# Sparse attention and token mixing on one core: another order for the products of weights and values, and one integer addition per decoded weight

## The chip, the cores and the metric

The kernel runs on one core of one Trainium2 chip, in one launch. The metric is the device time of that core in microseconds. The engines of a core are named as in the profile: PE is TensorE's matrix products and PEld its weight loads, DVE is VectorE, ACT is ScalarE, POOL is GpSimd, SP is SyncE, which here only issues DMAs.

## The reference

Two layers follow one another. The first is attention over 4 batches x 8 heads, 768 tokens, 64 channels per head, with a mask in blocks of 32 tokens: a query block sees its neighbours, the first and the last block, and three sampled ones; the first and the last query block see everything.

```python
scores = scale * np.matmul(q, k.transpose(0, 1, 3, 2))
scores = np.where(mask, scores, -1000000000.0)
scores = scores - np.max(scores, axis=-1, keepdims=True)
attn = np.exp(scores)
attn = attn / (np.sum(attn, axis=-1, keepdims=True) + 1e-09)
return np.matmul(attn, v).astype(np.float32)
```

Its output, 4 x 768 x 512, goes into a token mix:

```python
theta = x @ w_theta
zr, zi = x * np.cos(theta), x * np.sin(theta)
y = w_tok_r @ zr + w_tok_i @ zi        # over tokens, per batch
u = x + y
return (u + np.maximum(u @ w_ch, 0.0)).astype(np.float32)
```

The four weight matrices of the token mix arrive as float64, the rest as float32.

## The kernel before, in words

**Attention** (`attention`). The batches are taken in two halves `bp` of two batches. Per half there are 26 units: four "wide" ones, for the first and last query block against all keys, then one for each query block `i` from 1 to 22, against 8 key blocks. The engines' work is written out by hand in program order (`tc.manual_schedule`), a software pipeline over units `n`: in the turn of unit n come the key gathering of n+2 (`gather_k`, GpSimd copies, line 243), the scores of n+1 (`scores`, line 282, TensorE, and row minima on VectorE, line 285), the exponentials of n+1 (line 294, ScalarE), the transposes of n (line 300, TensorE) and their copy out of PSUM (line 302, ScalarE), and at every odd `i` the products of weights and values of the pair before it (`values`, line 335), whose results VectorE normalises (lines 315 to 319, one output tile `xo`) and SyncE stores to DRAM as `xs` (line 348). Last in a turn stand the loads of values: a window `va` (line 262, two buffers) and by `gather_v` an indirect DMA that GpSimd issues into one of four buffers `vb` (line 265). Queues are served in this order.

`values` works on a pair of query blocks and 16 heads (b, e, p). A head takes three products into its 64 rows of PSUM tile `X`: for each of the two query blocks one with the values of its sampled blocks, `vb`, 32 columns of weights wide; then one for both blocks with the shared window `va`, 64 columns wide, added to the two. Which rows of PSUM, and so which columns of the array, a head uses depends on p: rows 0 to 63 for even p, 64 to 127 for odd p. Each float32 product appears in the trace as two records. For the wide units `values_wide` (line 392) sums six products per head, 64 columns wide, two heads (c = 0 and 1) per call.

**Decoding of the weights** (`Piece`, `Decoder`). The float64 weights are read as pairs of 32-bit words and turned into two float32r parts, `hi` and `lo`. In the attention there are 22 pieces of 128 x 512, later 8 of 128 x 256 for `w_ch`. A piece has three phases. Before them ScalarE's `start` (line 63) scales the high word, read as float32, without its sign. `bits` (lines 67 to 69, VectorE) clips it, shifts it and puts the sign back: a float32 with the high word's part of the mantissa. `rest` (lines 75 and 77, VectorE) cuts out that value's power of two and multiplies the low word by it. Then ScalarE rounds the first part to `hi` (line 80), and `low` (lines 83 and 84, VectorE) subtracts `hi` and adds the rest. `Decoder.ahead` puts ScalarE's parts and `Decoder.go` the others into a turn. `attention` spreads the 66 phases over the units: none for the first two, then by a weight of 1 for a block and 2 for a wide unit, 56 in all. The load of piece k+2 (two buffers `raw`) is issued after `low` of piece k. In the turn, `go` stands behind the key gathering and ahead of the stores and the loads of values.

**Token mix** (`token_mix`). 48 steps in which weights' products with tokens (lines 584 to 586, angles; 622 to 624, mixing; 645 to 647, last product) fill TensorE. Here a planner orders the instructions. The last eight pieces are decoded in steps 1 to 12, two phases a step.

Of the kernel before, what the change touches and what calls it, by code (L numbers as in the profile page):

```python
# [10 lines left out]
F32 = mybir.dt.float32  # L11
F32R = mybir.dt.float32r
I32 = mybir.dt.int32
U32 = mybir.dt.uint32
AF = mybir.ActivationFunctionType
# [15 lines left out]

WORD_LO = float(np.array([768 << 20], np.uint32).view(np.float32)[0])
WORD_HI = float(np.array([(1022 << 20) | 0xFFFFF], np.uint32).view(np.float32)[0])
SIGN_BIT = -(1 << 31)
EXP_BITS = -(1 << 23)


C1 = 6.28125  # L40
# [5 lines left out]
class Piece:  # L46
# [13 lines left out]

    def start(self):
        self.a = self.pool.tile([P, self.f], F32, tag="da", name=f"da_{self.name}", bufs=2)
        self.nc.scalar.activation(self.a, self.raw[:, :, 1].bitcast(F32), AF.Abs, scale=2.0**-16)

    def bits(self):
        nc, a, ai = self.nc, self.a, self.a.bitcast(I32)
        nc.vector.tensor_scalar(a, a, WORD_LO, WORD_HI, op0=ALU.max, op1=ALU.min)
        nc.vector.tensor_scalar(ai, ai, 4, 1, op0=ALU.logical_shift_left, op1=ALU.logical_shift_right)
        nc.vector.scalar_tensor_tensor(ai, self.raw[:, :, 1], SIGN_BIT, ai, op0=ALU.bitwise_and, op1=ALU.bitwise_or)

    def rest(self):

        nc = self.nc
        s = self.pool.tile([P, self.f], I32, tag="ds", name=f"ds_{self.name}")
        nc.vector.tensor_scalar(s, self.a.bitcast(I32), EXP_BITS, None, op0=ALU.bitwise_and)
        low = self.raw[:, :, 0]
        nc.vector.scalar_tensor_tensor(low.bitcast(F32), low.bitcast(U32), 2.0**-52, s.bitcast(F32), op0=ALU.mult, op1=ALU.mult)

    def high(self):
        self.nc.scalar.copy(self.hi, self.a)  # L80

    def low(self):
        self.nc.vector.tensor_tensor(self.a, self.a, self.hi.bitcast(F32), op=ALU.subtract)
        self.nc.vector.tensor_tensor(self.lo, self.a, self.raw[:, :, 0].bitcast(F32), op=ALU.add)


class Decoder:
# [20 lines left out]
    def go(self, n):  # L108
        for k in range(self.at, min(self.at + n, 3 * len(self.pieces))):
            piece = self.pieces[k // 3]  # L110
            (piece.bits, piece.rest, piece.low)[k % 3]()
            if k % 3 == 2 and k // 3 + 2 < len(self.pieces):
                self.pieces[k // 3 + 2].load(self.pool, self.queue)
        self.at += n

# [54 lines left out]
def attention(tc, qT, qE, kT, vr, sampled, xs, ident, pieces, follow):  # L170
# [9 lines left out]
    with ExitStack() as ctx, ExitStack() as early:  # L180
# [146 lines left out]
        def values(bp, i):  # L327
            x = st[bp, i]["X"] = sums_tile(f"{bp}_{i}")
            va = vas[((i - 1) // 2) % VA_BUFS]
            order = [(b, e, p) for b in range(2) for e in range(2) for p in range(4)]  # L330

            def weigh(b, e, p, c, u0, n, v, start, stop):
                r0 = 64 * (p % 2) + 32 * u0
                v0 = 65 * (8 * b + 4 * (p // 2) + 2 * e + p % 2)
                nc.tensor.matmul(  # L335
                    x[r0 : r0 + 32 * n, b, 2 * (p // 2) + e, :], pT_pair[:, 4 * c + 2 * e + b, p, u0 : u0 + n, :], v[:, v0 : v0 + 65],
                    start=start, stop=stop,
                )

            for b, e, p in order:  # L340
                for u in range(2):
                    weigh(b, e, p, 1, u, 1, vbs[(i - 1 + u) % VB_BUFS], True, False)
                weigh(b, e, p, 0, 0, 2, va, False, True)

        def finish(bp, i):
            xo = normalised(f"{bp}_{i}", st.pop((bp, i))["X"], 8)
# [38 lines left out]
        def values_wide(bp, b, pp, e):  # L385
            if (b, pp, e) == (0, 0, 0):
                xws[bp] = sums_tile(f"w{bp}")
            x, v = xws[bp], vws[bp, b, pp]
            for c in range(2):
                for k in range(6):  # L390
                    v0 = 130 * e + 65 * c
                    nc.tensor.matmul(
                        x[64 * c : 64 * c + 64, b, 2 * pp + e, :], pT_wide[:, e, k, 64 * c : 64 * c + 64], v[:, k, v0 : v0 + 65],
# [389 lines left out]
```

## Time and profile before

| | |
|---|---|
| median of three runs | 726.09 us (721.34 to 729.16) |
| the profiled execution's own time | 730.01 us |
| its span, first to last instruction | 728.2 us |
| mean granted TensorE clock | 0.962 |
| moved by DMA | 95.57 MB, mean 131 GB/s |

The page of a profile gives each engine's busy time, and rows of forty digits, one for each fortieth of the span (18.2 us): the busy share of an engine in tenths, the clock that TensorE was granted, the mean share of the 16 DMA engines. The table by stage has the same in numbers for chosen stretches; its columns are the stretch, its length, each engine's busy time with the number of instructions, clock, DMA share and GB/s. The chain in order of time follows the work that ended last: start, length, engine, output tile and line. Timeline rows have the start, the length, engine, line, operation, output and inputs and the count of records merged into the row; a bracket behind it is the idle time before it and what ended that. Group rows have line, engine, operation, operands, shapes and count, then the busy time in us and the mean of one in ns, then the idle time ahead of them. Matrix products overlap, so the length of one is not the time that it costs.

### The profile page before, as it was taken

How to read it: one execution, taken by the hardware profiler on the slowest of the kernel's cores; microseconds unless marked ns; L12 is line 12 of the kernel's file. 1: busy time of each engine (PE TensorE's matmuls, PEld its weight loads, DVE VectorE, ACT ScalarE, POOL GpSimd, SP SyncE). 2: the span in 40 equal slices, each digit the busy share in tenths (PEclk: the TensorE clock that was granted, in tenths of full speed). 3: DMA queues.
4: the chain of work that ended last, by engine and by line, in shares of the span. 5: the costliest groups of instructions: out<-in, count | busy, mean ns of one | idle time of the engine just before them, and what ended most of it. 6: DMA issues, size and time to landing. Idle time of an engine off the chain costs nothing.

```text
span 728.2 us, 16678 instructions
## 1 busy us (share of the span) xinstructions
PE 681.6 (94%) x6592; PEld 566.3 (78%) x6592; DVE 462.2 (63%) x1063; ACT 333.8 (46%) x708; POOL 133.5 (18%) x262
## 2 busy tenths in 40 slices
PE   5899999997979999999785999999999999999997
PEld 2666666664666666666574999999999999999997
DVE  3676667563268575766427887875668575855753
ACT  3454545453155354535334556543554355633530
POOL 1435444432204444534000000000000000000000
PEclk9999999997589999999898999999999999999999
DMA  8665655866256564654324432242113311121102
GB/s 312 216 206 171 193 192 176 268 187 241 70 178 207 159 198 155 204 189 143 106 63 142 110 95 57 81 125 65 54 42 113 102 62 57 43 77 62 41 0 87
DMA packets 71110, 95.57 MB, mean 131 GB/s; under 512 B 5240, under 2 KB 52984, under 8 KB 71032
## 3 DMA queue, kind: packets, MB, share of 16 engines
q1 hardware_dynamic: 64696, 71.08, 30.9%
q0 software_dynamic: 6336, 23.43, 10.3%
q8 instruction: 52, 0.85, 0.5%
q14 instruction: 26, 0.21, 0.1%
HBM read 81.90 MB, written 12.58 MB: 130 GB/s over the span
## 4 chain that ended last, share of the span: by engine, by line
PE 69%; DMA 12%; DVE 10%; ACT 5%; SPq 2%; issue 2%; DVEq 0%; ACTq 0%
PE X L335 22%; PE y L622 7%; PE y L623 7%; PE y L624 7%; PE T L300 5%; DMA xs<-xo 3%; PE S L282 3%; DMA out_dram<-of 3%; PE SW L365 3%; ACT pT L302 3%; PE h L586 2%; PE h L584 2%; PE h L585 2%; DMA kb<-in_kT_dram 2%; PE o L645 2%; PE o L646 2%
## 5 line engine op out<-in xcount | busy, mean ns | idle before, releaser
L335 PE MATMUL X<-va,pT 128*64 128x65 f32 x704 | 118.4, 251 | 0.0
L335 PE MATMUL X<-vb,pT 128*32 128x65 f32 x1408 | 114.3, 236 | 1.5 <-ACT pT L302 1.1
L243 POOL COPY kg<-kb 128x256 f32 (+2 forms) x202 | 88.2, 477 | 67.8 <-PE S L282 33.8
L335 PEld LDWEIGHTS X<-va,pT 128*64 128x64 f32 x704 | 68.8, 138 | 34.2 <-issue 2.8
L302 ACT COPY pT<-T 128x1024 f32<-128x1024 f32 x44 | 44.6, 1014 | 96.7 <-PE T L300 96.5
L294 ACT ACTIVATE P<-S,m 128x256 f32<-128x256 f32 x176 | 69.1, 479 | 39.6 <-DVE m L285 39.6
L335 PEld LDWEIGHTS X<-vb,pT 128*32 128x32 f32 x1408 | 54.1, 109 | 35.3 <-ACT pT L302 1.3
L285 DVE TENSOR_REDUCE m<-S 128x2 f32<-128x512 f32 x88 | 56.4, 682 | 24.6 <-PE S L282 24.5
L265 POOL DMA_INDIRECT vb<-in_vr_dram,rows x44 | 43.3, 985 | 140.4 <-PE X L335 133.6
L622 PE MATMUL y<-w_tok_r_hi,zh 128*128 128x384 f32 x192 | 65.1, 339 | 2.8 <-DVE xo L319 1.6
L584 PE MATMUL h<-w_theta_hi,xTh 128*128 128x256 f32 x192 | 57.2, 298 | 10.5 <-ACT xTh L575 10.5
L623 PE MATMUL y<-w_tok_r_lo,zh 128*128 128x384 f32 x192 | 64.4, 335 | 0.0
L624 PE MATMUL y<-w_tok_r_hi,zl 128*128 128x384 f32 x192 | 64.2, 335 | 0.0
L623 PE MATMUL y<-w_tok_i_lo,zh 128*128 128x384 f32 x192 | 64.2, 334 | 0.0
L622 PE MATMUL y<-w_tok_i_hi,zh 128*128 128x384 f32 x192 | 64.2, 334 | 0.0
L624 PE MATMUL y<-w_tok_i_hi,zl 128*128 128x384 f32 x192 | 61.3, 334 | 0.0
L586 PE MATMUL h<-w_theta_hi,xTl 128*128 128x256 f32 x192 | 56.8, 297 | 1.4 <-DVE xTl L576 1.4
L585 PE MATMUL h<-w_theta_lo,xTh 128*128 128x256 f32 x192 | 56.4, 294 | 0.0
L300 PE MATMUL T<-ident,P 128*128 128x128 f32 x352 | 49.0, 283 | 4.0 <-ACT pT L302 1.6
L300 PEld LDWEIGHTS T<-ident,P 128*128 128x128 f32 x352 | 38.6, 143 | 15.9 <-ACT pT L302 13.7
L282 PE MATMUL S<-kg,q 64*32 64x256 f32 x1408 | 48.9, 387 | 0.0
L315 DVE TENSOR_SCALAR sm<-X 128x8 f32<-128x8 f32 x22 | 3.6, 165 | 70.1 <-PE X L335 70.1
(127 smaller groups left out, 1354.6 us busy)
## 6 DMA issues: line engine op xcount, KB each, us to landing
xa<-xs SPq DMA_DIRECT2D x192, 64.0 KB
vw<-in_vr_dram SPq DMA_DIRECT2D x8, 780.0 KB
kb<-in_kT_dram SPq DMA_DIRECT2D x8, 768.0 KB
xr<-xs SPq DMA_DIRECT2D x96, 64.0 KB
out_dram<-of SPq DMA_DIRECT2D x32, 192.0 KB
va<-in_vr_dram SPq DMA_DIRECT2D x22, 260.0 KB
q<-in_qT_dram SPq DMA_DIRECT2D x22, 256.0 KB
xs<-xo SPq DMA_DIRECT2D x44, 128.0 KB
```

The costliest lines, as they stand in the source:

```text
L243: nc.gpsimd.tensor_copy(dst, blocks.rearrange("r g s f -> r s g f"))
L282: nc.tensor.matmul(sc[32 * p : 32 * p + 32, e, b, :], q[rows, b, p, :], keys[rows, :, :, 4 * b + p, :], start=True, stop=True)
L294: nc.scalar.activation(pt[:, e, b, :], sc[:, e, b, :], AF.Exp, bias=m[:, e, b : b + 1], scale=-1.0)
L300: nc.tensor.transpose(t[:, k, :], pt, ident)
L302: nc.scalar.copy(out, t.rearrange("r k (p q) -> r k p q", p=4) if len(out.shape) == 4 else t)
L335: nc.tensor.matmul(x[r0 : r0 + 32 * n, b, 2 * (p // 2) + e, :], pT_pair[:, 4 * c + 2 * e + b, p, u0 : u0 + n, :], v[:, v0 : v0 + 65], star ...
L584: nc.tensor.matmul(ps, hi[:, c, :], wh[:, c, :], start=c == 0, stop=False)
L585: nc.tensor.matmul(ps, hi[:, c, :], wl[:, c, :], start=False, stop=False)
L586: nc.tensor.matmul(ps, lo[:, c, :], wh[:, c, :], start=False, stop=c == 3)
L622: nc.tensor.matmul(acc, zh[:, dd], wh[:, j, tt], start=j == 0 and m == 0, stop=False)
L623: nc.tensor.matmul(acc, zh[:, dd], wl[:, j, tt], start=False, stop=False)
L624: nc.tensor.matmul(acc, zl[:, dd], wh[:, j, tt], start=False, stop=j == 5 and m == 1)
```

## The change

Three things are changed.

In `values` the 16 heads are taken in four groups of four (one e, one half of p, both b and both p in it). In a group come first the eight products 32 wide, then the four 64 wide. The products are the same. In `values_wide` the loops over c and k are swapped, so that the two heads alternate.

In `Piece` a float32 value is made whole before it is split. ScalarE's `start` scales the high word by another power of two and has a second pass that scales the low word and writes it as an integer `r`. `bits` clips, shifts once, and puts the sign into `r`. `rest` is one integer addition by GpSimd of the two. `high` rounds the sum as before, and `low` is one subtraction. So VectorE's lines 75, 77 and 83 go, and ScalarE and GpSimd get one operation each. `r` has one buffer.

The load of piece k+2 is issued after `bits` of piece k, since nothing reads the raw words behind it.

```diff
-WORD_LO = float(np.array([768 << 20], np.uint32).view(np.float32)[0])
-WORD_HI = float(np.array([(1022 << 20) | 0xFFFFF], np.uint32).view(np.float32)[0])
+WORD_LO = float(np.array([512 << 20], np.uint32).view(np.float32)[0])
+WORD_HI = float(np.array([(766 << 20) | 0xFFFFF], np.uint32).view(np.float32)[0])
 SIGN_BIT = -(1 << 31)
-EXP_BITS = -(1 << 23)
...
-        self.nc.scalar.activation(self.a, self.raw[:, :, 1].bitcast(F32), AF.Abs, scale=2.0**-16)
+        self.nc.scalar.activation(self.a, self.raw[:, :, 1].bitcast(F32), AF.Abs, scale=2.0**-48)
+        self.r = self.pool.tile([P, self.f], I32, tag="ds", name=f"ds_{self.name}")
+        self.nc.scalar.activation(self.r, self.raw[:, :, 0].bitcast(U32), AF.Copy, scale=2.0**-29)
 
     def bits(self):
-        nc, a, ai = self.nc, self.a, self.a.bitcast(I32)
+        nc, a, ai, r = self.nc, self.a, self.a.bitcast(I32), self.r
         nc.vector.tensor_scalar(a, a, WORD_LO, WORD_HI, op0=ALU.max, op1=ALU.min)
-        nc.vector.tensor_scalar(ai, ai, 4, 1, op0=ALU.logical_shift_left, op1=ALU.logical_shift_right)
-        nc.vector.scalar_tensor_tensor(ai, self.raw[:, :, 1], SIGN_BIT, ai, op0=ALU.bitwise_and, op1=ALU.bitwise_or)
+        nc.vector.tensor_scalar(ai, ai, 3, None, op0=ALU.logical_shift_left)
+        nc.vector.scalar_tensor_tensor(r, self.raw[:, :, 1], SIGN_BIT, r, op0=ALU.bitwise_and, op1=ALU.bitwise_or)
 
     def rest(self):
 
-        nc = self.nc
-        s = self.pool.tile([P, self.f], I32, tag="ds", name=f"ds_{self.name}")
-        nc.vector.tensor_scalar(s, self.a.bitcast(I32), EXP_BITS, None, op0=ALU.bitwise_and)
-        low = self.raw[:, :, 0]
-        nc.vector.scalar_tensor_tensor(low.bitcast(F32), low.bitcast(U32), 2.0**-52, s.bitcast(F32), op0=ALU.mult, op1=ALU.mult)
+        ai = self.a.bitcast(I32)
+        self.nc.gpsimd.tensor_tensor(ai, ai, self.r, op=ALU.add)
...
     def low(self):
-        self.nc.vector.tensor_tensor(self.a, self.a, self.hi.bitcast(F32), op=ALU.subtract)
-        self.nc.vector.tensor_tensor(self.lo, self.a, self.raw[:, :, 0].bitcast(F32), op=ALU.add)
+        self.nc.vector.tensor_tensor(self.lo, self.a, self.hi.bitcast(F32), op=ALU.subtract)
...
-            if k % 3 == 2 and k // 3 + 2 < len(self.pieces):
+            if k % 3 == 0 and k // 3 + 2 < len(self.pieces):
                 self.pieces[k // 3 + 2].load(self.pool, self.queue)
...
-            order = [(b, e, p) for b in range(2) for e in range(2) for p in range(4)]
-
...
-            for b, e, p in order:
-                for u in range(2):
-                    weigh(b, e, p, 1, u, 1, vbs[(i - 1 + u) % VB_BUFS], True, False)
-                weigh(b, e, p, 0, 0, 2, va, False, True)
+            for e in range(2):
+                for pp in range(2):
+                    heads = [(b, e, 2 * pp + c) for b in range(2) for c in range(2)]
+                    for head in heads:
+                        for u in range(2):
+                            weigh(*head, 1, u, 1, vbs[(i - 1 + u) % VB_BUFS], True, False)
+                    for head in heads:
+                        weigh(*head, 0, 0, 2, va, False, True)
...
-            for c in range(2):
-                for k in range(6):
+            for k in range(6):
+                for c in range(2):
```

## The prediction

> **What bounds the kernel now.** I read the page first: who is busy, when, and at which clock.
>
> ```profile
> span 728.2 us, 16678 instructions
> PE 681.6 (94%) x6592; PEld 566.3 (78%) x6592; DVE 462.2 (63%) x1063; ACT 333.8 (46%) x708; POOL 133.5 (18%) x262
> ...
> PEclk9999999997589999999898999999999999999999
> DMA  8665655866256564654324432242113311121102
> ...
> PE 69%; DMA 12%; DVE 10%; ACT 5%; SPq 2%; issue 2%; DVEq 0%; ACTq 0%
> ```
>
> TensorE owns the chain that ended last. The table by stage then says where that can change.
>
> ```profile
> core 0: us, PE busy (x) PEld busy (x) DVE busy (x) ACT busy (x) POOL busy (x), PEclk, DMA share, GB/s
> 0.00:47.90 47.90, 35.62 (x449) 23.66 (x450) 29.13 (x71) 22.18 (x34) 16.75 (x45) 0.96 0.75 250
> ...
> 231.50:343.40 111.90, 110.70 (x1589) 73.58 (x1585) 73.34 (x122) 53.72 (x106) 50.42 (x94) 1.00 0.57 180
> ...
> 400.00:500.00 100.00, 98.80 (x608) 97.60 (x607) 77.45 (x232) 54.17 (x136) 0.00 (x0) 0.98 0.32 90
> 500.00:728.20 228.20, 222.86 (x1390) 222.49 (x1389) 145.84 (x371) 100.42 (x238) 0.00 (x0) 1.00 0.20 62
> ```
>
> From 400 us on, the token mix keeps TensorE busy 98% of the time with matrix products that the change doesn't touch: 328 us stay. The attention before it is a loop over pairs of query blocks, and the chain in order of time shows one period of it.
>
> ```profile
> 243.91 8.15 PE X L335 x96
> 252.06 1.04 PE T L300 x8
> 253.18 1.02 ACT pT L302
> 254.24 1.09 PE T L300 x8
> 255.33 1.02 PE S L282 x32
> 256.36 8.15 PE X L335 x96
> ```
>
> A period is 12.44 us (256.36 less 243.91): 8.15 for the 96 records of L335 (48 products of weights and values, each float32 product two records) and 4.3 for transposes and scores, TensorE hardly waiting. There are nine such periods in each of the two halves, 18 together.
>
> **The order of the products.** Within L335 the timeline, in narrow windows, reads:
>
> ```profile
> 111.21 0.25 PE L335 MATMUL X<-vb,pT 128*32 128x65 f32 x2
> ```
> ```profile
> 111.21 0.31 PE L335 MATMUL X<-vb,pT 128*32 128x65 f32 x4
> 111.44 0.33 PE L335 MATMUL X<-va,pT 128*64 128x65 f32 x2
> 111.70 0.31 PE L335 MATMUL X<-vb,pT 128*32 128x65 f32 x4
> ```
>
> One head is four records 32 columns wide, then two records 64 wide, and takes 0.49 us (111.70 less 111.21): 0.23 for the first kind, 0.26 for the second. The two products 32 wide go to different columns of the array and run side by side (both started within the first row's 0.25 us, and its two records end by 0.25, though one lasts 0.236 by the row below). Then the next width waits until the array has run empty. That is a switch of width twice per head, 32 times in the 8.15 us. The rows that show what the array does without such switches:
>
> ```profile
> 204.28 1.44 PE L392 MATMUL Xw<-vw,pT 128*64 128x65 f32 x24
> 205.65 0.33 PE L300 MATMUL Tw<-ident,PW 128*128 128x128 f32 x1
> ```
> ```profile
> 106.74 0.45 PE L282 MATMUL S<-kg,q 64*32 64x256 f32 x8
> ```
> ```profile
> L335 PE MATMUL X<-vb,pT 128*32 128x65 f32 x1408 | 114.3, 236 | 1.5 <-ACT pT L302 1.1 <-DVE xo L319 0.4
> L282 PE MATMUL S<-kg,q 64*32 64x256 f32 x1408 | 48.9, 387 | 0.0
> ```
>
> L392 puts 24 records of one width through in 1.37 us (205.65 less 204.28), 0.057 each, twelve after twelve on the same columns. And L282 shows eight records on eight parts of the array that all fit into 0.45 us, though one lasts 0.387: parts do run side by side.
>
> After the change four heads stand together: sixteen records 32 wide over four column groups (four per group instead of two), then eight 64 wide over two (four instead of two). Each stretch gets two more streams on its longest group: 0.23 + 2 x 0.057 = 0.35, and 0.26 + 0.11 = 0.37. Four groups of heads make 2.9 us instead of 8.0. From the other side: if no more than two column groups overlap, as the old rows show, the 32s take 0.23 + 6 x 0.057 = 0.58 and the 64s, one after another, 0.26 + 0.34 = 0.60, 4.7 in all. I take 3.0, near the lower end, because L282 overlaps eight. TensorE's own work per period falls from 12.44 to 7.3.
>
> L392's change of loops makes two column groups alternate: twelve steps of 0.057 and a run-out of about 0.15 are 0.85 us instead of 1.37.
>
> **What then sets the period.** Here another engine is near, so I sum each per period:
>
> ```profile
> 256.29:268.73 12.44, 12.31 (x184) 8.18 (x176) 7.73 (x13) 6.14 (x13) 5.92 (x13) 1.00 0.60 193
> 268.73:281.17 12.44, 12.31 (x184) 8.18 (x176) 9.15 (x16) 6.26 (x13) 5.65 (x13) 1.00 0.62 194
> sum 49.72, PE 49.19 PEld 32.72 DVE 32.77 ACT 24.07 POOL 21.81; mean PE 12.30 PEld 8.18 DVE 8.19 ACT 6.02 POOL 5.45
> ```
>
> The weights' decoding changes these. 66 phases over a weight of 56 give 2.36 phases, 0.79 pieces, per pair of blocks. Prices of a piece:
>
> ```profile
> L77 DVE SCALAR_TENSOR_TENSOR raw_tok_i<-raw_tok_i,ds_tok_i 128x512 f32<-128x512 uint32 x9 | 10.2, 1129 | 0.3
> L83 DVE TENSOR_TENSOR da_tok_i<-da_tok_i,w_tok_i_hi 128x512 f32<-128x512 f32 x9 | 6.6, 734 | 0.5 <-ACT w_tok_i_hi L80 0.5
> L63 ACT ACTIVATE da_tok_i<-raw_tok_i 128x512 f32<-128x512 f32 x9 | 6.1, 682 | 1.3 <-DMA raw_tok_i<-in_w_tok_i_dram 1.3
> L75 DVE TENSOR_SCALAR ds_tok_i<-da_tok_i 128x512 int32<-128x512 int32 x9 | 4.0, 443 | 0.0
> ```
> ```profile
> L243 POOL COPY kg<-kb 128x512 f32<-128x512 f32 x26 | 19.3, 751 | 34.0 <-DMA kb<-in_kT_dram 18.8 <-DMA q<-in_qT_dram 15.2
> ```
> ```profile
> L68 DVE TENSOR_SCALAR da_tok_r<-da_tok_r x9: 427/428/1749, 76.7 to 330.6; 128x512 int32<-128x512 int32 x9
> ```
>
> - VectorE loses lines 75, 77 and 83: 0.44 + 1.13 + 0.73 = 2.3 us a piece, 1.8 a period: 8.2 becomes 6.4. The rest keeps count and shape (the shift with one operation is put at its old price).
> - ScalarE gains one pass like L63, 0.68 a piece, 0.5 a period: 6.0 becomes 6.6.
> - GpSimd gains one addition with two inputs of 512. No row shows one; a copy with one input of 512 takes 0.75, two such reads 1.5. I take 1.1, the middle, 0.9 a period: 5.5 becomes 6.4. The copies and VectorE disturb each other (L68 takes 0.43 alone and up to 1.75), which the shorter period makes more frequent; I leave 0.5 for it.
> - The DMA engines must move what they moved in 12.44 us at a share of 0.61: 7.6 us at full share. The raw loads keep their number and come two phases earlier: SyncE's queue then waits at them for the clipping and shifting instead of the subtraction, and behind them stand the block's stores and the load of the next window of values, so nothing behind is later than before.
>
> The Trainium skill, GPSIMD Engine Reference, section 3.1, speaks against the move: it puts two-input arithmetic on GpSimd at about 2.6 cycles per element, twice VectorE's time. An estimate from it is 1.1 us for 512 elements, and the period's sum would be the same.
>
> The addition's wait: it stands in GpSimd's queue behind the gathers of keys and, in even blocks, behind a gather of values that waits for L335.
>
> ```profile
> POOL vb L265 <- PE X L335: 133.6, 19, 13.3
> ```
>
> That is 6 us of waiting per period, which goes as L335 gets shorter. Behind the addition wait ScalarE's rounding and VectorE's subtraction, and behind these the minima and exponentials. Most pieces take the subtraction one block later, 4 us in which the addition is long done, so I cost it at nothing; in the four blocks where both fall together a late addition can cost 1 to 2 us, within the margin below. In the token mix eight smaller additions (256 elements, up to 0.75 each) hide behind TensorE's 98.8 of 100 us; uncovered they would cost 6.
>
> So every resource needs 6.4 to 7.6 us, and the period can't be under 7.6. If the DMA engines are held at 0.75, their share over the longest dense stretch (the first row by stage), it is 7.6 / 0.75 = 10.1. Buffers let gathers land one and a half periods later, so I take **8.7**, a little under the middle, 3.74 less than before.
>
> **The sum,** against the profiled 728.2 us:
> - 18 periods x 3.74: -67.3.
> - Start to 47.9: one L392 at the low clock and two or three decode operations on the chain: -3.
> - The switch to the second half. Rows:
>
> ```profile
> 160.56 11.77 DMA kb<-in_kT_dram
> ...
> 182.99 12.34 PE X L335 x96
> ```
> ```profile
> 172.46 3.05 PE L365 MATMUL SW<-kb,qe 64*64 64x512 f32 x16 [3.12 <-DMA kb<-in_kT_dram]
> 175.44 1.97 PE L300 MATMUL T<-ident,P 128*128 128x128 f32 x8
> ```
>
> The 11.77 us for keys are a transfer and stay, so the shorter L335 ahead of 172.46 only makes that wait longer: 0. After it, TensorE runs at half clock and L335 takes 12.34; it falls to about 6: -6.3. Six L392 groups: -3.8. Lines 75, 77 and 83 once on the chain: -1.7.
> - Behind 343 two more L335 groups, one among other waits: -8. Weights of the last product, raw loads two phases earlier: -2.
>
> Together -92, a span of 636. The profiled execution's own time is 730.01, 1.8 above its span: **638 us**. It was 3.9 above the median 726.09, so the runs may lie some us below that.
>
> **The rivals.**
> 1. The queues overlap almost perfectly, the period is 7.6: 18 x 1.1 = 20 less, 618. For it: gathered values have four buffers, queries three. Against: TensorE, the DMA engines, ScalarE, VectorE and GpSimd would all be over 80% busy in queues kept in order. 0.2.
> 2. Column groups overlap only in twos: L335 at 4.7, the period about 9.5: 18 x 0.8 = 14 more, and 4 at the switch, 656. For it: the old rows show no more than two. Against: L282. 0.14.
> 3. The DMA engines bind at 0.75: period 10.1, 18 x 1.4 = 25 more, 663. For it: the digits of the page never stay over 8. 0.1.
> 4. The order does nothing (the width isn't what costs): L335 stays, only decoding gains, 722. Against: L392's 0.057 beside 0.49 / 6 = 0.083. 0.03.
> 5. Slower: the clock. TensorE idles 1.4 us per period where it idled none; after the 3.12 us wait above it ran at half clock (T 1.97 instead of 1.04). If every period brings that, 7.3 becomes 13.9, with the idle 15.3: 18 x 2.9 = 51 more than before, less 25, 756. It decides once the period passes 13.8 us. Against: a TensorE at half clock is also dense, which brings the clock back. 0.03. The Trainium skill, TensorE: Matmul & The Clock Gate, part 1, has the clock halve only after an idle window of some 3.4 us; by that rule this rival falls away, and the trace's 3.12 agrees roughly.
>
> **How the numbers follow.** The forecast has 0.5. The range 608 to 672 runs from a period of 7.6 with a switch 10 us better to 10.1 with one 9 us worse, takes in rivals 1 to 3 and leaves out 4, 5 and their margins. Faster by over 1% (what a measurement of this kernel can about tell from no change): 0.93; within 1%: 0.04, mostly rival 4; slower: 0.03.
>
> **What would show it.** Right: rows of L335 in groups of sixteen and eight, 96 records in about 3 us; a period near 8.7 with TensorE idle for 1 to 2 us of it; L392's 24 records in 0.85; DMA digits of 8 and 9 in the attention; the same 328 us at the end. Wrong: 96 records in 4.7 or more, PEclk digits of 5 to 7 in the periods, VectorE waiting for GpSimd's addition by microseconds in every period, or the store of results holding up VectorE's normalising.

## The result, and the profile after

The changed kernel takes 688.64 us (median of four, 685.89 to 692.51) against 724.68: a ratio of 0.950, interval 0.943 to 0.958. So it is faster, but by 36 us where 88 were forecast, and outside the range. Medians below are over all executions: two of the four of `spread` (635.4 and 637.3 us) count as slow beside the other two (625.6 and 630.4), and two executions far outside, 1133 us of the kernel before and 1760 us of `late_scale`, are left out of the ratios. The profiled execution took 689.56, its span is 687.8. Its page:

```profile
span 687.8 us, 16664 instructions
PE 573.4 (83%) x6592; PEld 498.1 (72%) x6592; DVE 403.0 (59%) x973; ACT 348.4 (51%) x738; POOL 167.3 (24%) x292
...
PEclk9999899886989998996989999999999999999999
DMA  8596767746398586742254322421124211121102
...
PE 41%; DMA 39%; DVE 12%; SPq 3%; ACT 2%; issue 2%; DVEq 0%; POOL 0%; ACTq 0%
```

TensorE lost 108 us of work, more than the forecast's whole gain, and the chain passed from it to the DMA engines (39% where it was 12%). Yet the digits of the DMA row are no higher than 7 or 8 for most of the attention. The list of waits, and the chain in order of time in the second half, say which transfer it is:

```profile
DVE xo L316 <- DMA xs<-xo: 78.8, 17, 12.0
...
POOL vb L262 <- PE X L330: 37.1, 13, 12.6
PEld X L330 <- DVE xo L316: 34.7, 13, 10.4
```
```profile
247.11 0.70 DVE xo L316
...
247.83 0.50 SPq L347
...
248.38 10.24 DMA xs<-xo
...
258.74 0.70 DVE xo L316
...
260.02 10.76 DMA xs<-xo
```

The period is now a ring of three: VectorE normalises into the one tile `xo` (0.70 us), SyncE's queue issues the stores, and the last of them lands 10 us later; only then may VectorE write `xo` again. TensorE's own part is as forecast. The timeline shows half the products of a pair of query blocks, sixteen and eight records in turn:

```profile
252.07 0.43 PE L330 MATMUL X<-vb,pT 128*32 128x65 f32 x16
252.44 0.45 PE L330 MATMUL X<-va,pT 128*64 128x65 f32 x8
252.82 0.43 PE L330 MATMUL X<-vb,pT 128*32 128x65 f32 x16
253.19 0.45 PE L330 MATMUL X<-va,pT 128*64 128x65 f32 x8
```

0.75 us from one group of four heads to the next (252.82 less 252.07), 3.0 for the 96 records. The table by stage, cut where the first group of a half and the tenth begin; its rows are the nine periods of the second half, the stretch between the halves, the rest, and the nine periods of the first half:

```profile
209.35:303.48 94.13, 73.78 (x1593) 51.41 (x1585) 48.99 (x97) 57.45 (x112) 58.08 (x101) 0.89 0.66 205
150.66:209.35 58.69, 42.03 (x657) 28.53 (x657) 31.12 (x54) 30.52 (x51) 22.07 (x34) 0.83 0.64 215
303.48:687.80 384.32, 353.13 (x2320) 348.46 (x2320) 246.44 (x663) 179.15 (x429) 8.22 (x9) 0.96 0.26 76
46.72:150.66 103.94, 72.33 (x1593) 50.13 (x1585) 51.82 (x98) 57.25 (x112) 60.70 (x104) 0.89 0.68 216
```

Nine periods are 103.9 and 94.1 us, 11.55 and 10.46 each, where 8.7 was forecast. No engine is busy for even 80% of them, and the DMA engines on the mean for 66 to 68%. That was the riddle: a store of 128 KB takes 10 us while a third of the DMA engines' time is free.

### The profile page after: what moved, and what is told of

Same layout as the page of the kernel before. It is cut to its first block, busy times and chain, and to the rows that moved or that the text cites. A ratio compares the mean times of both kernels' runs of the same rounds, so it can differ in the third digit from the quotient of the medians.

```text
span 687.8 us, 16664 instructions
## 1 busy us (share of the span) xinstructions
PE 573.4 (83%) x6592; PEld 498.1 (72%) x6592; DVE 403.0 (59%) x973; ACT 348.4 (51%) x738; POOL 167.3 (24%) x292
## 2 busy tenths in 40 slices
DMA packets 71110, 95.57 MB, mean 139 GB/s; under 512 B 5240, under 2 KB 52984, under 8 KB 71032
## 4 chain that ended last, share of the span: by engine, by line
PE 41%; DMA 39%; DVE 12%; SPq 3%; ACT 2%; issue 2%; DVEq 0%; POOL 0%; ACTq 0%
DMA xs<-xo 25%; PE y L621 7%; PE y L622 7%; PE y L623 7%; DMA out_dram<-of 3%; PE SW L364 3%; DMA xs<-xo_w 3%; PE h L583 3%; PE h L585 3%; DMA xr<-xs 2%; PE h L584 2%; PE o L644 2%; PE o L645 2%; PE o L646 2%; DMA kb<-in_kT_dram 2%; DMA raw_ch<-in_w_ch_dram 2%
## 5 line engine op out<-in xcount | busy, mean ns | idle before, releaser
L240 POOL COPY kg<-kb 128x256 f32 (+2 forms) x202 | 85.8, 467 | 15.3 <-DVE sb_raw L150 15.1
L330 PE MATMUL X<-vb,pT 128*32 128x65 f32 x1408 | 45.1, 247 | 28.6 <-DVE xo L316 27.6
L297 PE MATMUL T<-ident,P 128*128 128x128 f32 x352 | 52.1, 295 | 17.6 <-ACT pT L299 16.5
L282 DVE TENSOR_REDUCE m<-S 128x2 f32<-128x512 f32 x88 | 56.2, 679 | 13.2 <-PE S L279 13.2
L623 PE MATMUL y<-w_tok_i_hi,zl 128*128 128x384 f32 x192 | 63.0, 334 | 0.0
L316 DVE TENSOR_TENSOR xo<-X,sm 128x512 f32<-128x512 f32 x22 | 15.2, 691 | 81.6 <-DMA xs<-xo 78.8
L297 PEld LDWEIGHTS T<-ident,P 128*128 128x128 f32 x352 | 41.2, 150 | 29.6 <-ACT pT L299 26.7
L330 PEld LDWEIGHTS X<-vb,pT 128*32 128x32 f32 x1408 | 28.8, 121 | 45.8 <-DVE xo L316 34.7
L279 PE MATMUL S<-kg,q 64*32 64x256 f32 x1408 | 53.6, 417 | 9.3 <-POOL kg L240 6.1
L583 PEld LDWEIGHTS h<-w_theta_hi,xTh 128*128 128x128 f32 x192 | 38.0, 198 | 18.9 <-ACT P L291 14.4
L594 ACT ACTIVATE cs<-rr 128x256 f32<-128x256 f32 x48 | 19.8, 415 | 54.3 <-DVE rr L592 54.3
```

The lines of the kernel that those rows point to most:

```text
L240: nc.gpsimd.tensor_copy(dst, blocks.rearrange("r g s f -> r s g f"))
L279: nc.tensor.matmul(sc[32 * p : 32 * p + 32, e, b, :], q[rows, b, p, :], keys[rows, :, :, 4 * b + p, :], start=True, stop=True)
L282: nc.vector.tensor_reduce(m[:, e], sc[:, e], axis=AX.X, op=ALU.min)
L297: nc.tensor.transpose(t[:, k, :], pt, ident)
L330: nc.tensor.matmul(x[r0 : r0 + 32 * n, b, 2 * (p // 2) + e, :], pT_pair[:, 4 * c + 2 * e + b, p, u0 : u0 + n, :], v[:, v0 : v0 + 65], star ...
L583: nc.tensor.matmul(ps, hi[:, c, :], wh[:, c, :], start=c == 0, stop=False)
```

## The experiments

Medians in us; ratio to the kernel before, run beside it (medians 724.7 to 727.3). The periods are worked out from the profile of each run as above, for the first and the second half.

| run | median | ratio and interval | periods |
|---|---|---|---|
| the kernel before | 724.7 | | 12.47, 12.44 |
| the changed kernel | 688.6 | 0.950 (0.943 to 0.958) | 11.55, 10.46 |
| decode_only | 717.2 | 0.989 (0.985 to 0.993) | 12.50, 12.50 |
| order_only | 693.0 | 0.955 (0.947 to 0.962) | 11.17, 10.78 |
| q2 | 687.3 | 0.949 (0.944 to 0.954) | 11.16, 10.51 |
| xo2_q2 | 680.7 | 0.938 (0.932 to 0.945) | 11.12, 10.11 |
| xo2_q3 | 683.7 | 0.947 (0.939 to 0.955) | 10.72, 10.25 |
| store_act | 712.0 | 0.985 (0.977 to 0.992) | 12.62, 11.92 |
| no_raw | 675.6 | 0.932 (0.926 to 0.939) | 10.97, 9.78 |
| xo2_q3_no_raw | 663.3 | 0.916 (0.910 to 0.921) | 9.95, 9.26 |
| early_q | 687.5 | 0.946 (0.940 to 0.952) | 10.90, 10.29 |
| late_scale | 682.7 | 0.939 (0.932 to 0.946) | 10.69, 9.92 |
| early_q_late_scale | 685.0 | 0.944 (0.938 to 0.949) | 10.84, 10.33 |
| spread | 632.9 | 0.873 (0.864 to 0.882) | 8.88, 8.57 |
| before_spread | 704.7 | 0.969 (0.961 to 0.978) | 12.44, 12.44 |
| xo2_q2_spread | 630.1 | 0.868 (0.859 to 0.877) | 9.42, 8.51 |
| late_spread | 627.7 | 0.863 (0.853 to 0.873) | 8.74, 8.34 |
| four_stores | 636.1 | 0.877 (0.871 to 0.883) | 8.93, 8.72 |
| order_spread | 623.0 | 0.858 (0.852 to 0.864) | 9.78, 8.25 |
| decode_spread | 692.6 | 0.953 (0.948 to 0.959) | 12.45, 12.47 |

Five theories were tried on the missing gain. A: the single tile `xo` couples VectorE to the store's latency. F: the store stands behind other transfers in SyncE's queue. D: transfers are asked for too late. B: the sum of all bytes binds. E: the stores sit on a few of the 16 DMA engines, and these are full while the mean is not. The text behind a run's label was written before that run was made.

### The two parts alone

`decode_only` has the changed `Piece` and `values_wide` and the earlier raw loads, and the old loop in `values`. `order_only` is the kernel before with this in `values`:

```diff
-            for b, e, p in order:
-                for u in range(2):
-                    weigh(b, e, p, 1, u, 1, vbs[(i - 1 + u) % VB_BUFS], True, False)
-                weigh(b, e, p, 0, 0, 2, va, False, True)
+            for e in range(2):
+                for pp in range(2):
+                    heads = [(b, e, 2 * pp + c) for b in range(2) for c in range(2)]
+                    for head in heads:
+                        for u in range(2):
+                            weigh(*head, 1, u, 1, vbs[(i - 1 + u) % VB_BUFS], True, False)
+                    for head in heads:
+                        weigh(*head, 0, 0, 2, va, False, True)
```

decode_only: 

> The changed kernel with the old order of the products in values: the new decoding, the earlier raw loads and the swapped loops of the wide units alone. Theory A: TensorE sets the period again at 12.44 us, the store has 11 us to land and is not seen; only the wide units and the decoding on the chain gain, 715 to 724 us. Rival C: GpSimd's addition holds up others (its waits in the changed profile add up to over 100 us) and costs what the decoding gains: 725 to 735.

order_only: 

> The kernel before with the new order of the products in values alone. Theory A: the store's loop sets the period whatever the decoding does, 690 to 700 us, some 5 to 10 above the whole change. Rival C: without the additions in GpSimd's queue it is faster than the whole change, 675 to 687.

The order alone gives 693.0, within the intervals the whole gain. The rest alone gives 9 us and leaves the period at 12.50. The order's period, 11.17 and 10.78, is stretched by the same wait for the store (67.6 us in all), so the decoder isn't what keeps the gain away.

### More buffers (theory A)

`q2` has two query tiles instead of three, which makes room; `xo2_q2` a second `xo` beside. `xo2_q3` keeps three query tiles and makes the room by putting `r` into the raw words' own place, with the load of the next raw words one phase later.

```diff
-Q_BUFS = 3
+Q_BUFS = 2
...
-            xo = wp.tile([P, 8, 64], F32, tag="xo", name=f"xo{name}", bufs=1)[:, 0:n]
+            xo = wp.tile([P, 8, 64], F32, tag="xo", name=f"xo{name}", bufs=2)[:, 0:n]
```

`xo2_q3` has the second `xo` and:

```diff
-        self.r = self.pool.tile([P, self.f], I32, tag="ds", name=f"ds_{self.name}")
+        self.r = self.raw[:, :, 0]
...
-            if k % 3 == 0 and k // 3 + 2 < len(self.pieces):
+            if k % 3 == 1 and k // 3 + 2 < len(self.pieces):
```

xo2_q2: 

> The changed kernel with two output tiles xo in place of one (and two query tiles in place of three, which makes the room). Theory A: a period is a loop through the one tile (normalise 0.7, issue 0.5 to 1.0, store 8 to 11 us to land), and TensorE, DMA and the others need less. Then the wait of VectorE's line 316 for the store (78.8 us in total) all but goes, the periods fall from 10.5 to 11.5 to about 9, and the time to 640 to 665 us. Rival B: the store lands late because the DMA engines as a whole are full; then the wait moves to the queries, windows and gathered values, and the time stays at 675 to 690.

q2: 

> The control of the run before: the changed kernel with two query tiles in place of three and the one xo. Theory A: the query loads have slack while the store's loop sets the period, 686 to 694 us. Rival B: queries come later still and the time rises by some 5 to 15 us, to 693 to 703.

xo2_q3: 

> The changed kernel with two output tiles and all three query tiles; the room comes from keeping the low word's integer r in place in the raw words (so the raw load of piece k+2 goes behind the addition of piece k). In the run with two query tiles the wait only moved to queries (64.8 us) and windows (27 us). Theory A (too few tiles, each a loop through a transfer): with both kinds of tile free the periods fall to about 9, 650 to 667 us. Theory B (the transfers as a whole are late, since a period's 2.3 MB come in one burst at the end of the products): the wait moves on to windows and gathered values, 672 to 682.

The waits of `xo2_q2`:

```profile
DVE q L214 <- DMA q<-in_qT_dram: 64.8, 16, 11.4
...
PEld X L330 <- DMA va<-in_vr_dram: 28.6, 10, 9.5
...
PE X L330 <- DMA va<-in_vr_dram: 27.0, 10, 9.3
```

The wait of `xo` is gone, and 65 us of it have come back as waits for the queries, the next transfer in line, with more for the values. 680.7 is 8 us under the changed kernel, and the intervals overlap. With the third query tile back (`xo2_q3`) it is the same. Theory A falls as the cause: `xo` was only the first to notice.

### Another queue, earlier requests (theories F and D)

`store_act` lets ScalarE's queue issue the stores of `finish`:

```diff
-                nc.sync.dma_start(xs[bp, i : i + 2, c].rearrange("u q b p f -> u q (b p f)"), xo[64 * c : 64 * c + 64])
+                nc.scalar.dma_start(xs[bp, i : i + 2, c].rearrange("u q b p f -> u q (b p f)"), xo[64 * c : 64 * c + 64])
```

store_act: 

> The changed kernel with the stores of xo issued by ScalarE, so on a DMA queue of their own, one output tile. Theory F: the store waits in SyncE's queue behind the loads issued ahead of it; then it lands in 4 to 6 us in place of 8 to 11 and the time falls to 660 to 675. Theory B: the engines are full with the burst whichever queue asks; the store still needs 7 to 10, and 683 to 695 us.

It takes 712.0 us, more than the changed kernel and than both theories expected, and VectorE waits for the store as long as in the changed kernel (77.2 us against 78.8). The order within SyncE's queue wasn't it. Why the periods got longer, 12.62 and 11.92, was not followed up.

`early_q` is `xo2_q3` with the queries loaded one pair earlier; `late_scale` is `xo2_q3` with VectorE's scaling of the queries behind the decoder's phases, so that a late load holds up less (in both places where `go` stands; one is shown); the third run has both.

```diff
-            for i in (1, 3):
+            for i in (1, 3, 5):
...
-                if n + 4 < len(units) and not is_wide(n + 4) and units[n + 4][:2] not in ((0, 1), (0, 3)):
-                    load_q(*units[n + 4][:2])
+                if n + 6 < len(units) and not is_wide(n + 6) and units[n + 6][:2] not in ((0, 1), (0, 3), (0, 5)):
+                    load_q(*units[n + 6][:2])
...
-                do(n + 2, scale_q)
...
                     decoder.go(phases)
+                    do(n + 2, scale_q)
```

early_q: 

> The kernel with two output and three query tiles, the query load issued one pair earlier (line 452 asks for unit n+6 in place of n+4, so ahead of the stores and windows of its turn, not behind those of the turn before). In that kernel VectorE waited 60.1 us for queries. Theory D: the transfers are requested too late for where they are needed, and the period is request plus landing plus the work behind it; with the queries 4 to 5 us earlier their wait falls below 25 us and the time to 662 to 676. Theory B: the engines move what they can; the wait moves to windows, gathered values and stores, 678 to 688.

late_scale: 

> The kernel with two output and three query tiles, VectorE's scaling of the queries moved behind the decoding of its turn, so that row minima don't queue behind a query that has not landed (it is needed only one turn later). Theory D: 664 to 678 us. Theory B: 678 to 688.

early_q_late_scale: 

> Both moves of the queries together. Theory D: the queries' wait is gone and periods come to about 9, 655 to 670 us, with windows and gathered values as what is late next. Theory B: 676 to 688.

The waits of `early_q`:

```profile
PEld X L330 <- DMA va<-in_vr_dram: 35.1, 11, 7.6
PE X L330 <- DMA va<-in_vr_dram: 32.9, 11, 7.5
```

The wait for the queries is gone from the list, the one for the values has grown from 20 to 33 us, and the time has not moved. Three transfers in turn were each the late one. Asking earlier only changes whose turn it is: theory D falls too.

### Fewer bytes (theory B)

`no_raw` leaves out the load of the raw words for pieces 2 to 21 (they take those of an earlier piece), 10.5 of 95.6 MB; `xo2_q3_no_raw` does this to `xo2_q3`.

```diff
-                self.pieces[k // 3 + 2].load(self.pool, self.queue)
+                after = self.pieces[k // 3 + 2]
+                if after.f == 512:
+                    after.pool, after.raw = self.pool, piece.raw
+                else:
+                    after.load(self.pool, self.queue)
```

no_raw: 

> The changed kernel without the raw loads of pieces 2 to 21 (it leaves out 20 transfers of 512 KB, 10.5 MB of some 64 in the attention; the pieces are decoded from the first two tiles). One output tile. Theory B: a sixth less to move makes the store land 1.5 to 2 us sooner, periods of about 9, 655 to 672 us. Theory A in its narrow form (the store's own latency, whatever else moves): 683 to 690.

xo2_q3_no_raw: 

> Two output tiles, three query tiles and no raw loads of pieces 2 to 21 (left out as in the run before). Theory B: 15 to 25 us below the same kernel with the raw loads. Theory A: within 8 us of it, since no tile is short any more.

It helps, by 13 and 20 us, so transfers bind. But B alone doesn't close the books: with a ninth of all bytes gone VectorE waits for the store as long as before (81.0 us in `no_raw`), the time of `no_raw` is above B's range, and 9.78 us per period at a mean share of 0.62 is still far from full.

### Even stores (theory E)

What gave it away were narrow windows of the changed kernel, cut from a time in which the store of 260.02 (above) is under way:

```profile
260.50:261.00 0.50, 0.50 (x23) 0.35 (x20) 0.50 (x2) 0.28 (x1) 0.00 (x0) 1.00 0.11 45
...
266.00:266.50 0.50, 0.01 (x2) 0.00 (x0) 0.47 (x3) 0.38 (x2) 0.00 (x0) 1.00 0.54 216
266.50:267.00 0.50, 0.00 (x0) 0.00 (x0) 0.50 (x2) 0.50 (x3) 0.00 (x0) 1.00 0.14 53
267.00:267.50 0.50, 0.00 (x0) 0.00 (x0) 0.47 (x2) 0.50 (x2) 0.00 (x0) 0.64 0.12 50
267.50:268.00 0.50, 0.00 (x0) 0.00 (x0) 0.20 (x1) 0.50 (x2) 0.00 (x0) 0.50 0.12 50
```

The share falls to 0.12 and stays there: 0.12 x 16 is 1.9. Two engines work, at 50 GB/s together, and fourteen have nothing to do, while TensorE stands idle and waits. The single packets in the trace say the same: between 266.5 and 268 us there are 30 of them, and nearly all lie in two sequences in which each packet begins about when the one before it ends (2,048 bytes, the size of a store's row, in 84 ns; 4,160 bytes, that of a gather's row, in 161 ns). From 260.2 to 261.7 us it is 24 packets in two such sequences, and most of them have the size of a gather's row or of a raw load's (4,096 bytes): the two engines are behind with all that they are given, not only with the stores. A store writes 64 rows of `xo` to two blocks of `xs`, a pattern of 2 x 32 rows whose two groups lie far apart. `spread` changes the order of the DRAM tile, so that the same 64 rows lie in one even run; number and bytes of the stores stay.

```diff
-    xs = dram.tile([NP, NB, 2, 32, 2, 2, P], F32, name="xs")
+    xs = dram.tile([NP, 2, NB, 32, 2, 2, P], F32, name="xs")
...
-                nc.sync.dma_start(xs[bp, i : i + 2, c].rearrange("u q b p f -> u q (b p f)"), xo[64 * c : 64 * c + 64])
+                nc.sync.dma_start(xs[bp, c, i : i + 2].rearrange("u q b p f -> (u q) (b p f)"), xo[64 * c : 64 * c + 64])
...
-                src = xs[b // 2, 4 * j : 4 * j + 4, p % 2, :, b % 2, p // 2]
+                src = xs[b // 2, p % 2, 4 * j : 4 * j + 4, :, b % 2, p // 2]
```

The other uses of `xs` follow suit. Three more runs do this to the kernel before, to `xo2_q2` and to `late_scale`.

spread: 

> The changed kernel with the parts of the DRAM tile xs in another order (the half c ahead of the block), so that a store of 64 rows of 2 KB is one even run of 64 rows where it was two groups of 32 rows far apart. Bytes, number of stores and queue stay. Theory E (a store in two groups is served by two of the 16 DMA engines, which have their share of every other transfer beside it; the mean share of 0.66 to 0.68 hides that these two are full): the store takes under 5 us where it took 8 to 15, the wait of VectorE for it falls from 79 us in all to below 25, the nine periods come to 10.3 us or less in the first half and 9.3 or less in the second (11.55 and 10.46), the time to 655 to 672 us. Theory B (the sum of the bytes binds, however they are spread): periods and time stay, 684 to 692 us.

before_spread: 

> The kernel before with the same other order of xs. Theory E: its period of 12.44 us was set by TensorE's order of products and its stores took no part, so the time stays within 6 us of 726; theory B the same. If it falls by more than 10 us, the stores bound the kernel before as well, and the change of order was not worth what it showed.

xo2_q2_spread: 

> xo2_q2 (two tiles xo, two q) with the other order of xs. Theory E: the waits for q (65 us) and va (28 us) fall to less than half as well, since they stood in the same two engines behind the stores; periods of 9.5 or less and 8.8 or less, 650 to 666 us. Theory B: 677 to 685 us as xo2_q2 (680.7).

late_spread: 

> late_scale (two xo, three q, the sum of the weight's words in the raw words, scaling of q behind the decoder) with the other order of xs. Theory E: the shortest of all, 645 to 662 us, periods of 8 to 9 us near the 8.7 of the forecast. Theory B: 679 to 686 us as late_scale (682.7).

`spread` takes 632.9 us, 56 less than the changed kernel, far below what either theory expected. Its page, its list of waits and its table by stage:

```profile
PEclk9989899888989999878999999999999999999999
DMA  8599989993699899725542134111242111211002
```
```profile
DVE xo L316 <- DMA xs<-xo: 7.6, 6, 2.9
```
```profile
181.16:258.33 77.17, 68.28 (x1592) 47.24 (x1584) 57.82 (x101) 57.31 (x112) 60.11 (x102) 0.99 0.91 264
128.24:181.16 52.92, 40.01 (x664) 26.63 (x656) 28.57 (x50) 31.00 (x53) 21.32 (x34) 0.88 0.71 229
258.33:623.80 365.47, 348.33 (x2326) 345.23 (x2320) 244.82 (x659) 179.16 (x429) 8.23 (x9) 0.98 0.27 79
```

The wait for the store went from 78.8 to 7.6 us, the DMA row now has its eights and nines, the share in the periods is 0.91, and these last 8.88 and 8.57 us. TensorE is busy for 68.3 of 77.2. Theory E holds, and B may hold now, as the bound that is left; no run took bytes out of this kernel to test that. In the kernel before the period didn't move (12.44), as expected, but it gained 20 us, which wasn't expected: 14 in the last part and 6.5 between the halves. So uneven transfers had cost it time too, outside its periods. By the expectation a fall of more than 10 us spoke against the test; since the nine periods stood still, it doesn't for them, and the run below with the old order of `xs` settles it. The three runs with the changed products ended 17 to 22 us below theory E's ranges, about as much as the kernel before gained. With even stores the other buffers and the later scaling bring nothing that the intervals show (630.1 and 627.7).

`four_stores` cuts each store in two of 32 rows and leaves `xs` as it was, to tell the stores from the loads of the last part, which read the new order.

```diff
-                nc.sync.dma_start(xs[bp, i : i + 2, c].rearrange("u q b p f -> u q (b p f)"), xo[64 * c : 64 * c + 64])
+                for u in range(2):
+                    nc.sync.dma_start(xs[bp, i + u, c].rearrange("q b p f -> q (b p f)"), xo[64 * c + 32 * u : 64 * c + 32 * u + 32])
```

four_stores: 

> The changed kernel with each store of 64 rows cut into two of 32 rows, each within one block; the DRAM tile and the loads of the second part are as they were. If the even stores alone make the periods short, these come to 8.6 to 9.2 us as in spread (8.88 and 8.57). The last 366 us of spread were 19 us shorter than those of the changed kernel (384): if this came from the loads that read the other order of xs, the tail here stays at 380 to 386 and the time is 645 to 656 us; if from the stores, the time is 629 to 638 us.

The periods are short again, 8.93 and 8.72, with twice the number of stores: it was the uneven split of a store, not the place in DRAM. The part from the second half's tenth group on takes 372.2 us, between the 384.3 of the changed kernel and the 365.5 of `spread`: by these single executions some 12 come from the stores and 7 from the loads. The counts of packets, a line of each page, agree to the packet; changed kernel, `four_stores`, `spread` and `no_raw`:

```profile
DMA packets 71110, 95.57 MB, mean 139 GB/s; under 512 B 5240, under 2 KB 52984, under 8 KB 71032
```
```profile
DMA packets 72430, 95.58 MB, mean 151 GB/s; under 512 B 6560, under 2 KB 54304, under 8 KB 72352
```
```profile
DMA packets 74030, 95.58 MB, mean 153 GB/s; under 512 B 8160, under 2 KB 55904, under 8 KB 73952
```
```profile
DMA packets 68229, 85.08 MB, mean 126 GB/s; under 512 B 4920, under 2 KB 52664, under 8 KB 68152
```

From the first line to the second 1320 packets under 512 B come in while the bytes stay: these belong to the way in which a transfer is carried out, not to its data. The Trainium skill, DMA: Bandwidth & Descriptors, section "Why a DMA increments its semaphore by 16 and not by 1", says why: each engine that takes part closes with a write to the semaphore, and their number is the largest up to 16 that divides the slowest dimension of both sides. By that rule a raw load of 128 rows has 16: leaving out 20 should take away 320, and 5240 less 4920 is 320. A store of 2 x 32 rows has two: 88 stores of 16 in place of 44 of two are 1320 more, and 6560 less 5240 is 1320. In `spread` 44 stores go from 2 to 16 (616) and the 192 loads `xa<-xs`, four blocks each, from 4 to 16 (2304): 2920, and 8160 less 5240 is 2920. The trace agrees with the rule in every case.

### The two parts with even stores

`order_spread` and `decode_spread` are `order_only` and `decode_only` with the order of `xs` of `spread`, by the same edit.

order_spread: 

> The kernel before with the new order of products in the values and the other order of xs, without the change of the decoder. Theory P (the order alone carries the gain, as the forecast had it, with the decoder a few us): periods of 8.6 to 9.4 us, 632 to 648 us. Rival V: VectorE's work of decoding then binds, periods of 9.8 us or more and 650 us or more.

decode_spread: 

> The changed kernel with the old order of products in the values and the other order of xs: the period stays at 12.4 us, bound by TensorE's products, and the time lies 0 to 12 us under the 704.7 of before_spread (decode_only lay 9 under the kernel before): 692 to 705 us. A time under 685 us would show that the decoder's part carries more than the forecast gave it.

The order alone takes 623.0 us, the lowest of all; the decoder without it 692.6, 12 under `before_spread`. With the order in, the decoder's change brings nothing more. Whether it costs something (632.9 and 627.7 with it, 623.0 without) stays open, since the intervals touch. `order_spread` missed its expectation too: it is 9 us below theory P's range, with periods of 9.78 and 8.25 on either side of P's 8.6 to 9.4; why the first half's are longer was not followed up. In the second half VectorE, with all its old decoding, is busy for 67.73 of 74.26 us, so the room that the decoder's change makes on VectorE wasn't needed there:

```profile
184.13:258.39 74.26, 67.03 (x1592) 46.78 (x1584) 67.73 (x122) 53.35 (x106) 58.45 (x94) 1.00 0.91 272
```

## Why the prediction was wrong

The stretches of the profiled executions, in us. The last two columns are the change measured where the stores are even, `spread` less `before_spread`.

| stretch | before | forecast | after less before | `before_spread` | `spread` less it |
|---|---|---|---|---|---|
| to the first group | 47.8 | -3 | -1.1 | 45.8 | +2.5 |
| nine periods, first half | 112.3 | -33.7 | -8.4 | 111.9 | -31.9 |
| between | 71.4 | -11.8 | -12.7 | 64.9 | -12.0 |
| nine periods, second half | 111.9 | -33.7 | -17.8 | 111.9 | -34.8 |
| the rest | 384.8 | -10 | -0.5 | 370.7 | -5.2 |
| sum | 728.2 | -92 | -40.4 | 705.2 | -81.4 |

- **TensorE's products: right.** 3.0 for L335 was taken near the lower end because L282 overlaps eight parts, and 3.0 it is; the 4.7 of rival 2 is out. L392, now L391, was put at 0.85, and 0.85 it is (180.48 less 179.63):

```profile
179.63 0.92 PE L391 MATMUL Xw<-vw,pT 128*64 128x65 f32 x24
180.48 1.77 PE L364 MATMUL SW<-kb,qe 64*64 64x512 f32 x16
```

- **The engines per period: right within 5%,** read from `spread`, where nothing else stretches them (a ninth of its first row above): VectorE 6.4 (forecast 6.4), ScalarE 6.4 (6.6), GpSimd 6.7 (6.4), TensorE 7.6 (7.3), the DMA engines at full share 7.8 (7.6). GpSimd's addition was between 0.75 and 1.5, at 1.1, and takes 1.3 (in the token mix 0.87, where up to 0.75 was put). A group of the changed kernel:

```profile
L75 POOL TENSOR_TENSOR da_tok_i<-da_tok_i,ds_tok_i 128x512 int32<-128x512 int32 x9 | 11.7, 1300 | 39.1 <-DVE ds_tok_i L70 32.1 <-ACT w_tok_i_hi L78 6.9
```

ScalarE, next in line, waited for it 0.5 us in these nine pieces and 4.1 us in all 22 of the attention, so its place behind the gathers cost little; the forecast had it at nothing, and 1 to 2 us in four blocks in its margin:

```profile
L78 ACT CAST w_tok_i_hi<-da_tok_i 128x512 fp32r<-128x512 f32 x9 | 5.8, 644 | 0.5 <-POOL da_tok_i L75 0.5
```

The estimate of 1.1 by the Trainium skill, GPSIMD Engine Reference, section 3.1, is 0.2 below what the row shows.

- **The step that failed: "The DMA engines must move what they moved in 12.44 us at a share of 0.61: 7.6 us at full share".** It treats 16 engines as one. Two of them carry every store of `finish` alone, as the narrow windows and the counts of packets show. The two stores of a pair of query blocks, 262 KB at the 50 GB/s of the narrow windows, take 5.2 us; the other bytes, 10.46 us x 205 GB/s less 262 KB, are 1.88 MB, at the 290 GB/s that `spread` reaches at full share (264 / 0.91) 6.5 us. Together 11.7 us for these two: an estimate, a tenth above the 10.46 measured and far over the 7.6 of the mean. By the same sum they were nearly full in the kernel before (12.1 of its 12.44, from 180 GB/s), when hardly a wait showed it (5.8 us for the store in all). So the 8.7 could not come, and the term built on it fell short: -67.3 became -26.2. Where the stores are even it is -66.7.

The Trainium skill, Perfetto Trace Analysis, section 'What "DMA-bound" means', puts single DMA engines first among what a DMA-bound kernel can be bound on. The prediction read only the mean; the narrow windows of this case show two engines at work while the others rest.

- **The other rivals:** 1 (618) needed a period of 7.6, which these two engines did not allow and even stores did not reach (8.57), and 4 and 5 are out: the order does carry the gain, and the kernel is faster.

- **Rival 3 came nearest,** and not for its reason. It had the DMA engines bind at a mean share of 0.75, with a period of 10.1; they bound at 0.66 to 0.68, with 11.55 and 10.46. The share of 0.75 in the first stretch was no limit: `spread` reaches 0.91.

- **The sign named as wrong did appear:** the store holding up VectorE's normalising. The prediction had looked at SyncE's order and found nothing behind it later; the transfer itself was not sized.

- **The switch: right in sum,** -12.7 against -11.8, and in part by luck: the group of products there was to fall from 12.34 us to about 6 and takes 3.61 (177.01 less 173.40), so the other terms gave 4.0 where 5.5 was forecast.

```profile
173.40 0.66 PE L330 MATMUL X<-vb,pT 128*32 128x65 f32 x16
...
177.01 0.87 PE L297 MATMUL Tw<-ident,PW 128*128 128x128 f32 x6
```

- **The end: missed.** The two last groups were to give 8 us; instead they stood behind transfers. The chain of the changed kernel:

```profile
304.63 8.61 DMA va<-in_vr_dram
...
315.27 3.27 DMA xr<-xs
```

With even stores the same stretch gives 5.2.

- **The clock: small.** TensorE's clock fell to 0.89 on the mean in the second half's periods, from 1.00, since it idles there; rival 5 named the mechanism, but TensorE was not the bound, so little hung on it (the last section has more on the clock). In `spread` it is 0.99 in the second half.

That `spread` ends near the forecast's 638 is in part chance: 20 of its us come from stores and loads in other stretches that the kernel before lost too.

## What to carry to other kernels

Before a mean DMA share is turned into time, look at how each transfer is laid out: one whose outermost dimension is 2 runs on two engines here, and they fill up while the mean reads 0.6. Windows of half a microsecond in which the share stands at a small multiple of 1/16, and the count of the smallest packets per transfer, show it in a profile. When a freed wait only moves to the next transfer, stop adding buffers and ask which engine all those transfers share.

## What the runs showed of the hardware beside this

TensorE's clock fell after less idling than the prediction's 3.12 us. In the narrow windows above it is idle from about 266.0 on and its clock is halved within the window that ends at 267.50: 0.64 on the mean, so from 267.14 on, 1.1 us later. It had stood still a little before as well:

```profile
263.50:264.00 0.50, 0.39 (x4) 0.15 (x2) 0.00 (x0) 0.00 (x0) 0.50 (x2) 1.00 0.64 193
264.00:264.50 0.50, 0.00 (x0) 0.00 (x0) 0.17 (x1) 0.00 (x0) 0.50 (x3) 1.00 0.53 115
264.50:265.00 0.50, 0.09 (x8) 0.12 (x16) 0.50 (x2) 0.00 (x0) 0.50 (x1) 1.00 0.86 232
```

Two idle pieces, 1.0 and 1.1 us, within 3.3 us were enough here. It is not the only case: the clock's record in this trace has 18 such falls ahead of the end, and in 13 of them the longest idle piece of TensorE in the 6 us before was shorter than 3.12 us (1.1 to 3.1). Nor did the prediction's own row need its whole wait, which began at 169.34 us (172.46 less 3.12):

```profile
171.00:172.50 1.50, 0.04 (x1) 0.07 (x2) 0.00 (x0) 0.53 (x1) 0.00 (x0) 0.75 0.81 332
```

A mean of 0.75 here is half the window at full clock and half at 0.50, so the clock fell at 171.75, after 2.4 us. So the last ground on which the prediction set rival 5 aside, the length of the wait, does not hold in these traces. How much idling is enough was not tested.
